# A packed attention and channel-mix kernel: the first sequence's second softmax by token, its mixing on TensorE, and another order of the first loads

## The chip, the cores and the metric

One core of a Trainium2 chip runs the whole program. Its engines work through instruction lists of their own: TensorE (PE; matmuls, with weight loads shown as PEld), VectorE (DVE), ScalarE (ACT), GpSimd (POOL) and SyncE (SP), which here issues all DMA transfers. The metric is the device time of one execution in microseconds; less is better.

## The reference

Batch 8, 8 heads, 576 tokens, head size 64, 32 packed queries p; d_model 512, d_ff 1024. All data is 32-bit float, except the weights w_k, w_v, w_r, which come in 64 bits.

```python
def sm_attn(qq, kk, vv):
    s = scale * np.matmul(qq, kk.transpose(0, 1, 3, 2))
    s = s - np.max(s, axis=-1, keepdims=True)
    a = np.exp(s)
    a = a / (np.sum(a, axis=-1, keepdims=True) + 1e-09)
    return np.matmul(a, vv)
p_packed = sm_attn(p, k, v)
x = sm_attn(q, p_packed, p_packed)          # heads side by side: 512 columns
...
xk = mu_k * x + (1.0 - mu_k) * x_prev       # x_prev: x one token earlier, 0 at the first
xr = mu_r * x + (1.0 - mu_r) * x_prev
k = np.maximum(xk @ w_k, 0.0)
v = k * k @ w_v
r = 1.0 / (1.0 + np.exp(-(xr @ w_r)))
return (r * v)
```

## The kernel before

The channel mix walks over 9 tiles of 512 tokens. For each it does gates (xr by w_r, L717 to L719), keys (xk by w_k, L678 to L680) and values (squared keys by w_v, L746 to L748): 48, 96 and 96 matmuls, since each operand is kept as a high and a low float32r half and a product takes three matmuls. Below, three matmuls of this kind are a group. Weights arrive as 64-bit blocks of 128 rows and 512 columns (`st`, 0.524 MB) and go through `convert`: ACT scales the upper words (L285), DVE puts the bits together (L287 to L291), ACT rounds to the high half (L295), DVE subtracts for the low half (L297). There are 4 blocks of w_r, 8 of w_k and 8 of w_v.

The attention of the 8 sequences is laid between these matmuls. A sequence b loads k, v, q (`raw`, `vt`, `vl`) and p (`pin`); for b = 0 and 1, k and q are transposed on PE (L387). `front` makes the first softmax and the packed keys `pm`; `back` does the second softmax with heads and packed positions on the partitions, in two halves of the tokens: scores (L541), a transpose of 32x32 blocks (L553), maximum, subtraction, exp, sum and division by packed position (L560 to L572), a transpose back (L576), and the product with `pm` (L584). `mixed_in` copies x to `xt`, and `mix` makes xr and xk: ACT scales x (L639), DVE adds the scaled x one token earlier (L643), ACT rounds (L659), DVE subtracts (L661).

The order on every engine is fixed at build time by a planner, the class `Flow`. Each piece of work is a generator that yields (engine, duration, ready time); `Flow.run` always takes the piece that could start first by its own cost figures, with a `rank` to decide ties. SP's list, and so the order of the transfers, comes out of the same planner. While the first tile is not ready, the planner fills PE with matmuls of no use (L817, `spare`). Buffers come from numbered slots, and an instruction that needs a slot waits for the last reader of the slot before.

## Time and profile before

| | us |
|---|---|
| runs | 605.92, 607.71, 608.11 |
| median | 607.71 |
| profiled execution, span from first to last instruction | 605.1 |
| PE, DVE, ACT busy in it | 593.7, 363.9, 331.0 |

The profiled execution's own device time is not given apart from its span. Times in the rows below are us from the span's start. Matmuls overlap at their ends: one of 512 columns is shown with 0.39 us, but in a stream a new one starts every 0.2275 us. A float32 matmul has two records, a transpose one.

### The profile page before, as it was taken

How to read it: one execution, taken by the hardware profiler on the slowest of the kernel's cores; microseconds unless marked ns; L12 is line 12 of the kernel's file. 1: busy time of each engine (PE TensorE's matmuls, PEld its weight loads, DVE VectorE, ACT ScalarE, POOL GpSimd, SP SyncE). 2: the span in 40 equal slices, each digit the busy share in tenths (PEclk: the TensorE clock that was granted, in tenths of full speed). 3: DMA queues.
4: the chain of work that ended last, by engine and by line, in shares of the span. 5: the costliest groups of instructions: out<-in, count | busy, mean ns of one | idle time of the engine just before them, and what ended most of it. 6: DMA issues, size and time to landing. Idle time of an engine off the chain costs nothing.

```text
span 605.1 us, 10174 instructions
## 1 busy us (share of the span) xinstructions
PE 593.7 (98%) x3984; PEld 471.1 (78%) x3984; DVE 363.9 (60%) x701; ACT 331.0 (55%) x579; POOL 2.1 (0%) x23
## 2 busy tenths in 40 slices
PE   8899999999999999999999999999999999999997
PEld 7787777777777777777877787778788888888886
DVE  1499999949688479556765577166503822451321
ACT  4478784775774648454845485457534803641420
POOL 0000000000000000000000000000000000000000
PEclk9899999999999999999999999999999999999999
DMA  8895561764634646346034702000010010001001
GB/s 189 248 266 136 216 155 34 166 126 88 113 60 137 118 70 139 99 74 143 1 103 64 144 1 72 20 1 0 26 45 1 0 70 0 2 0 71 0 2 69
DMA packets 159184, 49.43 MB, mean 82 GB/s; under 512 B 143776, under 2 KB 151968, under 8 KB 159136
## 3 DMA queue, kind: packets, MB, share of 16 engines
q1 hardware_dynamic: 159136, 48.79, 34.0%
q8 instruction: 31, 0.51, 0.3%
q14 instruction: 17, 0.14, 0.1%
HBM read 39.33 MB, written 9.44 MB: 81 GB/s over the span
## 4 chain that ended last, share of the span: by engine, by line
PE 84%; DVE 5%; ACT 4%; SPq 3%; DMA 2%; issue 1%; ACTq 0%
PE pvo L746 11%; PE ph L678 10%; PE pvo L747 10%; PE pvo L748 10%; PE ph L680 10%; PE ph L679 10%; PE pr L717 5%; PE pr L719 5%; PE pr L718 5%; SPq L207 3%; PE pa L461 2%; PE pa L584 2%; DMA st<-in_moe_w_r 1%; PE pa L541 1%; ACT x L639 1%; DVE m L289 1%
## 5 line engine op out<-in xcount | busy, mean ns | idle before, releaser
L678 PE MATMUL ph<-xk,wk_h 128*128 128x512 f32 x288 | 114.8, 399 | 0.0
L746 PE MATMUL pvo<-wv_h,sq 128*128 128x512 f32 x288 | 113.9, 395 | 0.0
L679 PE MATMUL ph<-xk,wk_h 128*128 128x512 f32 x288 | 112.4, 390 | 0.0
L680 PE MATMUL ph<-xk,wk_l 128*128 128x512 f32 x288 | 112.3, 390 | 0.0
L747 PE MATMUL pvo<-wv_l,sq 128*128 128x512 f32 x288 | 112.3, 390 | 0.0
L748 PE MATMUL pvo<-wv_h,sq 128*128 128x512 f32 x288 | 112.2, 390 | 0.0
L689 ACT ACTIVATE r<-ph 128x512 f32<-128x512 f32 x72 | 43.0, 598 | 90.7 <-PE ph L680 89.7
L696 DVE CAST sq<-r 128x512 fp32r<-128x512 f32 x72 | 30.3, 420 | 100.6 <-ACT r L692 98.4
L746 PEld LDWEIGHTS pvo<-wv_h,sq 128*128 128x128 f32 x288 | 54.1, 188 | 15.9 <-issue 4.5
L678 PEld LDWEIGHTS ph<-xk,wk_h 128*128 128x128 f32 x288 | 54.1, 188 | 15.5 <-issue 4.5
L643 DVE SCALAR_TENSOR_TENSOR x<-xt,mus,x 128x512 f32<-128x512 f32 (+7 forms) x128 | 60.4, 513 | 6.0 <-ACT x L639 5.9
L680 PEld LDWEIGHTS ph<-xk,wk_l 128*128 128x128 f32 x288 | 54.1, 188 | 11.5
L748 PEld LDWEIGHTS pvo<-wv_h,sq 128*128 128x128 f32 x288 | 54.1, 188 | 11.4
L639 ACT ACTIVATE x<-xt,mus 128x512 f32<-128x512 f32 (+7 forms) x128 | 62.0, 530 | 1.5 <-DVE xr L661 1.3
L747 PEld LDWEIGHTS pvo<-wv_l,sq 128*128 128x128 f32 x288 | 54.1, 188 | 10.7
L679 PEld LDWEIGHTS ph<-xk,wk_h 128*128 128x128 f32 x288 | 54.2, 188 | 10.3
L717 PE MATMUL pr<-wr_h,xr 128*128 128x512 f32 x144 | 58.7, 408 | 0.0
L719 PE MATMUL pr<-wr_h,xr 128*128 128x512 f32 x144 | 56.7, 394 | 1.0 <-DVE xr L661 1.0
L718 PE MATMUL pr<-wr_l,xr 128*128 128x512 f32 x144 | 56.3, 391 | 0.0
L728 ACT ACTIVATE sig<-pr 128x512 f32<-128x512 f32 x36 | 21.3, 601 | 60.1 <-PE pr L719 56.5
L698 DVE TENSOR_TENSOR sq<-r,sq 128x512 fp32r<-128x512 f32 x72 | 49.4, 686 | 1.4
L757 DVE TENSOR_TENSOR sig<-pvo,sig 128x512 f32<-128x512 f32 x36 | 23.9, 686 | 38.8 <-PE pvo L748 38.8
(80 smaller groups left out, 727.5 us busy)
## 6 DMA issues: line engine op xcount, KB each, us to landing
out<-sig SPq DMA_DIRECT2D x36, 256.0 KB, 2.1
vt<-in_v SPq DMA_DIRECT2D x16, 512.0 KB, 4.6
raw<-in_k SPq DMA_DIRECT2D x96, 72.0 KB, 2.8
raw<-in_q SPq DMA_DIRECT2D x96, 72.0 KB, 2.8
st<-in_moe_w_k SPq DMA_DIRECT2D x8, 512.0 KB, 6.0
st<-in_moe_w_v SPq DMA_DIRECT2D x8, 512.0 KB, 5.5
raw<-in_k SPq DMA_DIRECT2D x16, 144.0 KB, 2.9
raw<-in_q SPq DMA_DIRECT2D x16, 144.0 KB, 5.1
```

What stands on the lines that cost most here:

```text
L639: nc.scalar.mul(x32[:, o:o + n], xts[b, c][:, 1 + s:1 + s + n], mus[:, j, c:c + 1])
L643: nc.vector.scalar_tensor_tensor(x32[:, o:o + n], xts[b, c][:, s:s + n], mus[:, j + 1, c:c + 1], x32[:, o:o + n], op0=ALU.mult, op1=ALU.add,)
L678: nc.tensor.matmul(ph, wk_h[:, c, fs], xh, start=(c == 0), stop=False)
L679: nc.tensor.matmul(ph, wk_h[:, c, fs], xl, start=False, stop=False)
L680: nc.tensor.matmul(ph, wk_l[:, c, fs], xh, start=False, stop=(c == NC - 1))
L698: nc.vector.tensor_tensor(hl[:, 1, :], r, hl[:, 0, :].bitcast(F32), op=ALU.subtract)
L717: nc.tensor.matmul(pr, xh[:, ts_], wr_h[:, c, :], start=(c == 0), stop=False)
L718: nc.tensor.matmul(pr, xh[:, ts_], wr_l[:, c, :], start=False, stop=False)
L719: nc.tensor.matmul(pr, xl[:, ts_], wr_h[:, c, :], start=False, stop=(c == NC - 1))
L746: nc.tensor.matmul(pv[t], sh, wv_h[:, f, :], start=(f == 0), stop=False)
L747: nc.tensor.matmul(pv[t], sh, wv_l[:, f, :], start=False, stop=False)
L748: nc.tensor.matmul(pv[t], sl, wv_h[:, f, :], start=False, stop=(f == NF - 1))
```

## The change

For sequence 0 the second softmax puts tokens on the partitions: `both` holds the packed keys of each pair of heads apart, scores come out as 128 tokens by 8 heads by 32 positions (`by_token`), the softmax runs along the free dimension (`weights_by_token`, three windows of 256, 256 and 64 tokens), and PE transposes the weights to `A0`. Then xr and xk of tile 0 come straight from PE: `shared` multiplies `pm` by mu and 1 - mu, and `first_mix` adds the product with `A0` and that with `A0` one token earlier in PSUM, 256 tokens at a time; `first_out` rounds and subtracts from there. The 64 tokens that belong to tile 1 are kept aside.

The planner's constants change the order of the loads. Blocks of weights have buffers of their own (`st`, 8); the split w_v is written over its own block; w_k's conversions wait for the last window of `A0` (`held`). The shares mu are loaded as rows and transposed on PE for the later tiles, and broadcast to 32 partitions for sequence 0; those loads and sequence 0's pins are issued on POOL.

```diff
-    FIRST = 10.09, 10.29
+    FIRST = 9.985, 9.995, 9.997, 10.06
...
+        if beside:
+            yield "gpsimd", 1.0, None, None
+            nc.gpsimd.dma_start(dst, src)
+            return
...
+        if held:
+            yield from flow.wait(("A", 2))
...
+        if hi is None:
+            wv = wvs[c] = tile_([P, 2, DM], F32R, "st", slot, "wv")
+            h, l = wv[:, 0, :], wv[:, 1, :]
...
+    def by_token(sb2, both):
...
+                    nc.tensor.matmul(
+                        s2[:n, j, :, 32 * pr:32 * pr + 32], ts["qT", 0, pr][1][:, t:t + n], both[:, :, pr, :],
+                        start=True, stop=True,
+                    )
...
+    def weights_by_token(w, blocks, slot, s2):
...
+        nc.vector.tensor_reduce(m2, sc, axis=AX.X, op=ALU.max)
+        nc.vector.tensor_tensor(e, sc, m2.unsqueeze(3).broadcast_to([n, nb, 8, 32]), op=ALU.subtract)
+        nc.scalar.activation(e, e, AF.Exp, scale=scale)
+        nc.vector.tensor_reduce(z2, e, axis=AX.X, op=ALU.add)
...
+        nc.vector.tensor_tensor(e, e, z2.unsqueeze(3).broadcast_to([n, nb, 8, 32]), op=ALU.mult)
...
+        nc.scalar.copy(parts["A0"][:, :, 1 + t:1 + t + total], tp[:, :, :total])
...
+    def first_mix():
...
+                for tap in range(2):
+                    for pr in (2 * g, 2 * g + 1):
+                        own = slice(32 * pr, 32 * pr + 32)
+                        for h, half in enumerate(HALVES):
+                            o = 1 - tap + t
+                            nc.tensor.matmul(
+                                px[half, pr % 2, :n], pms[own, j, tap, h * D:(h + 1) * D], A[own, h, o:o + n],
+                                start=(tap == 0), stop=(tap == 1),
+                            )
...
+    def first_out(tag, j, w, g, slot, px, tiles, kept):
...
+            nc.scalar.copy(tiles[c][:, 0, cols], px[:, c % 2, :n])
+            nc.vector.tensor_tensor(tiles[c][:, 1, cols], px[:, c % 2, :n], tiles[c][:, 0, cols].bitcast(F32), op=ALU.subtract)
```

SP's list at the first loads, before (`st` are weight blocks, `mus` the shares, `pin` the p of the next sequence):

```order
L207 DMA vt<-in_v 128x4x256
L207 DMA vl<-in_v 64x4x64
L207 DMA raw<-in_q 96x6x64 x8
L207 DMA st<-in_moe_w_r 128x1024 x2
L207 DMA mus<-in_moe_mu_k 128x4x1
L207 DMA mus<-in_moe_mu_r 128x4x1
L207 DMA st<-in_moe_w_r 128x1024 x2
L207 DMA pin<-in_p 32x4x32 x3
L207 DMA st<-in_moe_w_k 128x1024
```

And SP's list now, from the last of sequence 0's k on:

```order
L212 DMA st<-in_moe_w_r 128x1024
L212 DMA vt<-in_v 128x4x256
L212 DMA vl<-in_v 64x4x64
L212 DMA vt<-in_v 128x4x256
L212 DMA vl<-in_v 64x4x64
L212 DMA st<-in_moe_w_r 128x1024 x2
L212 DMA raw<-in_q 96x6x64 x8
L212 DMA st<-in_moe_w_r 128x1024
L212 DMA by_row<-in_moe_mu_k 4x128
L212 DMA by_row<-in_moe_mu_r 4x128
L212 DMA st<-in_moe_w_k 128x1024 x8
L212 DMA pin<-in_p 32x4x32 x4
```

Three blocks of w_r moved ahead of q, all of w_k ahead of the next sequence's pins, and sequence 0's own pins left SP.

DVE's list at the end of the second softmax of sequence 0, now (`et` are weights by token, `m2t` their maxima and sums, `pt` the transposed pins of sequence 1):

```order
L657 TENSOR_REDUCE m2t<-s2t 64x8
L669 RECIPROCAL m2t<-m2t 128x16
L659 TENSOR_TENSOR et<-s2t,m2t 64x256
L671 TENSOR_TENSOR et<-et,m2t 128x512
L665 TENSOR_REDUCE m2t<-et 64x8
L752 TENSOR_TENSOR xr<-pa,xr 128x256
L667 TENSOR_SCALAR m2t<-m2t 64x8
L425 STREAM_TRANSPOSE pt<-pin 128x128
L752 TENSOR_TENSOR xr<-pa,xr 128x256 x2
L669 RECIPROCAL m2t<-m2t 64x8
L671 TENSOR_TENSOR et<-et,m2t 64x256
L752 TENSOR_TENSOR xr<-pa,xr 128x256 x4
```

Before, that transpose (L416) stood far behind, among the keys; now it stands between the first subtractions of xr (L752).

PE's list at the first gates, now (L731 is the mixing product, L677 the transposes of the weights):

```order
L731 MATMUL pa<-A_403,pms 64x256 x16
L677 MATMUL tpt<-ident,et 128x128 x4
L1022 MATMUL spare<-ident 128x128 x4
L731 MATMUL pa<-A_403,pms 64x256 x8
L897 MATMUL pr<-wr_h,xr 128x512
L898 MATMUL pr<-wr_l,xr 128x512
L899 MATMUL pr<-wr_h,xr 128x512
L731 MATMUL pa<-A_403,pms 64x256 x8
L677 MATMUL tpt<-ident,et 128x64 x2
L897 MATMUL pr<-wr_h,xr 128x512
```

Mixing products now stand between the groups of gates, where fillers stood; sequence 1's transposes of k, which all came before the gates, now come among the last gates and the first keys.

## Rows read from the trace of the kernel before

**Rows 1.** The page, parts 1 and 2: busy time of every engine, and TensorE's busy tenths in 40 slices of 15.1 us.

```profile
PE 593.7 (98%) x3984; PEld 471.1 (78%) x3984; DVE 363.9 (60%) x701; ACT 331.0 (55%) x579; POOL 2.1 (0%) x23
...
PE   8899999999999999999999999999999999999997
```

**Rows 2.** The table of stages (busy us of each engine and instructions in a stretch, granted TensorE clock, busy share of the DMA engines, GB/s), for the scaling stage of tile 0 and for the end of its values.

```profile
40.00:50.00 10.00, 9.02 (x73) 8.06 (x72) 9.93 (x17) 9.82 (x19) 0.00 (x0) 1.00 0.99 267
100.00:120.00 20.00, 20.00 (x140) 14.70 (x139) 20.00 (x41) 13.72 (x29) 0.10 (x1) 1.00 0.51 120
```

**Rows 3.** PE's timeline from the last transposes of sequence 0's keys to the scores of sequence 1 (start, us, instruction, idle time before it in brackets with its releaser).

```profile
7.62 0.69 PE L387 MATMUL pa<-ident,raw 96*128 96x96 f32 x6 [0.18 <-DMA raw<-in_k]
...
44.67 0.48 PE L717 MATMUL pr<-wr_h,xr 128*128 128x512 f32 x1
...
48.56 2.39 PE L817 MATMUL spare<-ident 128*128 128x128 f32 x20
...
52.33 0.48 PE L717 MATMUL pr<-wr_h,xr 128*128 128x512 f32 x1
...
61.57 0.39 PE L678 MATMUL ph<-xk,wk_h 128*128 128x512 f32 x1
...
70.56 1.21 PE L437 MATMUL pa<-kT,pt 64*32 64x288 f32 x32 [1.34 <-DVE pt L416]
```

**Rows 4.** The line that issues all loads, L207, in three stretches: durations of the issue (min/median/max in ns), first and last start, and the time from issue to landing (the last pin of sequence 0; the last two pieces of q; all pieces of q to 60 us).

```profile
L207 SPq DMA_DIRECT2D pin<-in_p x1: 429/429/429, 6.5 to 6.5; - x1
...
DMA to landing us min/median/max: 1.7/1.7/1.7
...
L207 SPq DMA_DIRECT2D raw<-in_q x2: 429/468/506, 16.4 to 16.9; - x2
...
DMA to landing us min/median/max: 2.9/3.6/4.2
...
L207 SPq DMA_DIRECT2D raw<-in_q x14: 376/518/3148, 9.5 to 46.2; - x14
```

**Rows 5.** The table of stages for the time of the loads; the last two columns are the busy share of the DMA engines and GB/s.

```profile
10.00:15.00 5.00, 4.50 (x50) 3.86 (x34) 1.94 (x6) 2.29 (x6) 0.00 (x0) 1.00 0.96 236
15.00:20.00 5.00, 3.35 (x57) 2.98 (x57) 0.00 (x0) 1.96 (x6) 0.00 (x0) 0.82 0.85 180
20.00:30.00 10.00, 10.00 (x140) 8.76 (x139) 6.70 (x13) 4.94 (x12) 0.00 (x0) 0.92 0.88 285
24.00:26.00 2.00, 2.00 (x42) 1.45 (x27) 1.97 (x3) 0.94 (x2) 0.00 (x0) 1.00 1.00 404
```

**Rows 6.** ACT's timeline while q arrives: the copy of the transposed packed keys, the first step of a weight block, and a copy of a half of q.

```profile
22.64 0.28 ACT L485 COPY ppT<-pa 128x128 f32<-128x128 f32 x1
22.80 0.69 ACT L285 ACTIVATE m<-st 128x512 f32<-128x512 f32 x1
23.37 0.41 ACT L392 COPY qT<-pq 128x288 f32<-128x288 f32 x1
```

**Rows 7.** DVE's timeline: the transpose of sequence 0's pins, two maxima of the second softmax, a subtraction and two scaled additions of the mixing, and the first and last step of one w_k block.

```profile
8.34 0.31 DVE L416 STREAM_TRANSPOSE pt<-pin 128x128 f32<-128x128 f32 x1 [8.34 <-DMA pin<-in_p]
...
26.68 1.37 DVE L560 TENSOR_REDUCE m<-e 128x18 f32<-128x576 f32 x2
...
45.61 0.69 DVE L661 TENSOR_TENSOR xr<-x,xr 128x512 fp32r<-128x512 f32 x1
...
49.34 1.41 DVE L643 SCALAR_TENSOR_TENSOR x<-xt,mus,x 128x512 f32<-128x512 f32 x2
...
55.28 0.42 DVE L287 TENSOR_SCALAR m<-m 128x512 uint32<-128x512 uint32 x1
...
57.07 0.68 DVE L297 TENSOR_TENSOR wk_l<-m,wk_h 128x512 fp32r<-128x512 f32 x1
```

**Rows 8.** PE's timeline at two places where small matmuls stand inside the stream: three transposes of q among the keys, and one output product of sequence 1 among the values (16 records are 8 matmuls).

```profile
76.36 0.39 PE L680 MATMUL ph<-xk,wk_l 128*128 128x512 f32 x1
76.59 0.41 PE L387 MATMUL pa<-ident,raw 96*128 96x96 f32 x3
...
77.10 0.40 PE L679 MATMUL ph<-xk,wk_h 128*128 128x512 f32 x1
...
101.60 0.39 PE L748 MATMUL pvo<-wv_h,sq 128*128 128x512 f32 x1
101.92 0.74 PE L584 MATMUL pa<-a,pm 32*64 32x288 f32 x16
...
102.92 0.40 PE L747 MATMUL pvo<-wv_l,sq 128*128 128x512 f32 x1
```

**Rows 9.** The table of stages around the wait for q; the third column from the end is the granted clock as a share of 2.4 GHz.

```profile
14.00:16.00 2.00, 0.49 (x5) 0.23 (x3) 0.00 (x0) 0.60 (x2) 0.00 (x0) 1.00 0.44 98
16.00:17.00 1.00, 0.35 (x3) 0.28 (x3) 0.00 (x0) 0.00 (x0) 0.00 (x0) 1.00 1.01 229
19.00:20.00 1.00, 1.00 (x8) 0.92 (x6) 0.00 (x0) 0.60 (x3) 0.00 (x0) 0.50 0.84 163
22.00:23.00 1.00, 1.00 (x13) 1.00 (x11) 0.00 (x0) 0.94 (x4) 0.00 (x0) 1.00 0.72 178
```

**Rows 10.** The timeline of all engines at the first gates of tile 1: the subtraction that makes the last xr tile, and the matmul that reads it.

```profile
120.23 0.69 DVE L661 TENSOR_TENSOR xr<-x,xr 128x512 fp32r<-128x512 f32 x1
...
121.06 0.41 PE L719 MATMUL pr<-wr_h,xr 128*128 128x512 f32 x1
```

More of the change, by code (lines that the diff above doesn't have):

```diff
@@ L213, in attn_pack_channel_mix @@
     LANDS = 2.0
+    WLOAD = 2.6e-3
     T6 = S // 6
@@ L482, in front @@
         nc.tensor.transpose(pT[:, :P], pm.rearrange("p a b -> p (a b)"), ident)
+        if b == 0:
+            s2 = yield from flow.take("a2")
+            both = tile_([P, 2, NPR, 32], F32, "a2", s2, "ppB")
+            nc.gpsimd.memset(both, 0.0)
+            yield act(2 * P)
+            for h, own in enumerate(HALVES):
+                nc.scalar.copy(both[own, h], pT[own, :P].rearrange("p (r x) -> p r x", x=32))
+            flow.give("pa", slot)
+            flow.spawn(shared(sp, pm), RANK_MIX)
+            parts["A"] = yield from flow.take("xt")
+            A = parts["A0"] = tile_([P, 2, S + 1], F32, "xt", parts["A"], "A0")
+            nc.gpsimd.memset(A[:, :, 0:1], 0.0)
+            flow.spawn(by_token(s2, both), rank(b) - 1)
+            return
         ppT = sb.tile([P, P], F32, name="ppT", tag="ppT")
@@ L593, in back @@
             flow.spawn(mixed_in(b, hf, g, slots[g], px[g]), rank(b, hf) - 1)
+    parts = {}
+    WINDOWS = (0, 256), (256, 256), (TB, S - TB)
+    def by_token(sb2, both):
+        yield from flow.wait(*(("qT", 0, pr) for pr in range(NPR)))
+        todo = []
+        for w in range(3):
+            slot = yield from flow.take("m")
+            s2 = ps.tile([P, 2, 2, P], F32, name="s2t", tag=f"m{slot}")
+            blocks = [(t, min(P, S - t)) for t in range(256 * w, min(256 * w + 256, S), P)]
+            yield pe(0.55 * len(blocks))
+            for j, (t, n) in enumerate(blocks):
+                for pr in range(NPR):
+                    nc.tensor.matmul(
+                        s2[:n, j, :, 32 * pr:32 * pr + 32], ts["qT", 0, pr][1][:, t:t + n], both[:, :, pr, :],
+                        start=True, stop=True,
+                    )
+            flow.spawn(weights_by_token(w, blocks, slot, s2), rank(0) - 1 + 0.001 * w if w < 2 else RANK_MIX + 0.02)
+        for pr in range(NPR):
+            flow.give("kq", ts.pop(("qT", 0, pr))[0])
+        flow.give("a2", sb2)
@@ new lines, in shared @@
+    def shared(sp, pm):
+        yield from flow.wait("mub")
+        ss = yield from flow.take("sig")
+        parts["pms"] = ss
+        pms = parts["pm"] = tile_([P, 2, 2, 2 * D], F32, "sig", ss, "pms")
+        flat = pm.rearrange("p a b -> p (a b)")
+        for j in (1, 0):
+            yield vec(P)
+            nc.vector.tensor_tensor(pms[:, j, 0], flat, mub[1][:, j], op=ALU.mult)
+            yield vec(P)
+            nc.vector.tensor_tensor(pms[:, j, 1], flat, pms[:, j, 0], op=ALU.subtract)
+        flow.give("pm", sp)
+        flow.give("sig", mub[0])
+        flow.set("pms")
@@ L629, in mix @@
         for c in range(NC):
-            yield from flow.wait(*(("xt", b, c, hf) for b, *_ in pieces(i) for hf in range(2)))
+            yield from flow.wait(*(
+                e for b, *_ in pieces(i)
+                for e in ([("xt", b, c, 0), ("xt", b, c, 1)] if b else [("kept", j // 2, c // 2)])
+            ))
             slot = yield from flow.take("xk" if tag == "xk" else "sq")
-            space = "sig" if i == 0 else "tmp"
+            space = "tmp"
             sx = yield from flow.take(space)
@@ L666, in attn_pack_channel_mix, with made @@
     sqs, sigs = {}, {}
+    def made(tag, i, c, t=NT - 1):
+        if i:
+            return [(tag, i, c)]
+        return [(tag, 0, c, hf) for hf in range(1 + (t >= 2))]
     def keys(i):
@@ L712, in gates @@
             for c in range(NC):
-                yield from flow.wait(("xr", i, c), *(("wr", c, o) for o in range(0, DM, WP)))
+                yield from flow.wait(*made("xr", i, c, t), *(("wr", c, o) for o in range(0, DM, WP)))
                 yield pe(0.69)
@@ L785, in all_loads @@
             yield from loads(b)
+    mub = []
     def shares():
-        for j, mu in ((0, mu_k), (2, mu_r)):
-            yield from load(mus[:, j, :], mu.rearrange("(c p) -> p c", p=P), 0.46, 0.23)
+        sm = yield from flow.take("sig")
+        mub[:] = sm, tile_([P, 2, 2 * D], F32, "sig", sm, "mub")
+        for j, mu in ((0, mu_k), (1, mu_r)):
+            for pr in range(NPR):
+                yield from load(
+                    mub[1][32 * pr:32 * pr + 32, j, :],
+                    mu[2 * D * pr:2 * D * (pr + 1)].unsqueeze(0).broadcast_to([32, 2 * D]), 0.46, 0.05, beside=True,
+                )
+        flow.now.t += 2.5
+        flow.set("mub")
+        flow.now.t = 0.0
+        flow.now.rank = RANK_SHARES
+        sr = yield from flow.take("tmp")
+        by_row = tile_([2 * NC, P], F32, "tmp", sr, "by_row")
+        for j, mu in ((0, mu_k), (1, mu_r)):
+            yield from load(by_row[NC * j:NC * (j + 1), :], mu.rearrange("(c p) -> c p", p=P), 0.46, 0.05)
             if not j:
                 back_to_issue()
+        slot = yield from flow.take("pa")
+        pT = banks(slot).rearrange("p a b -> p (a b)")
+        yield pe(0.1)
+        nc.tensor.transpose(pT[:, :2 * NC], by_row, ident[:2 * NC, :2 * NC])
+        flow.give("tmp", sr)
+        yield act(2 * NC)
+        nc.scalar.copy(mus[:, 0::2, :], pT[:, :2 * NC].rearrange("p (a b) -> p a b", a=2))
+        flow.give("pa", slot)
         yield vec(2 * NC)
```

144 lines of the change are left out of this document (113 added, 31 removed).

## The prediction

> **What bounds the kernel now.** Five views, in this order. The page says TensorE is busy 98% of the span, with full digits from slice 3 on [rows 1]. The table of stages adds that DVE is full from 40 to 50 us and still at 100 to 120 us, while PE loses little [rows 2]. So from some moment on PE is a stream that nothing interrupts, and the end lies one stream behind that moment. PE's timeline finds it [rows 3]: gates of tile 0 begin at 44.67 us, but by 52.33 only three groups of three matmuls are done, with fillers between; from there groups follow at one matmul in 0.2275 us, and keys begin at 61.57. In the keys one wait of 1.34 us stands before the scores of sequence 1. I therefore compare "start of keys, plus what PE loses after it": before, 61.57 + 1.34 = 62.9 us. Everything behind (tiles 1 to 8, the tail) is the same work, so a microsecond here is one at the end, unless DVE turns late.
>
> **Arrival of the data.** The first 25 us wait for loads. The last of k was there at 7.6 [rows 3], the pins at 6.5 + 1.7 = 8.2, the last of q at 16.9 + 4.2 = 21.1 [rows 4]; these 12.9 us carried v and q, 1.18 MB each. At the rates of the windows around (236 and 180 GB/s, [rows 5]) it would be 5.0 + 6.6 = 11.6. I take 12.2. A weight block has 0.524 MB: 1.3 us at the best window's 404 GB/s, 1.84 at the 285 of 20 to 30 us [rows 5]; I take 1.3, because that window carried mostly weights. Afterwards three w_r blocks come before the end of q: 8.2 + 3.9 + 12.2 = 24.3 us (23.7 to 26.6), the fourth at 25.6. Eight w_k blocks (10.4) and the pins of sequence 1 (0.6 before, 0.7 here) put those pins at 36.7 us (36.1 to 43.9). I leave the small loads moved to POOL in the place of the old pins.
>
> **The chain after q.** On ACT the first step of w_r's last block stands before the last copy of q: 25.6 + 0.6 + 0.4 = 26.6 us [rows 6]. Then the scores by token run; DVE needs the first eight products. The fillers, 128 columns wide, pass at 0.12 a record, two records to a product [rows 3]; with 64 columns I put a product between 0.12 and 0.24, so the eight end at 27.6 to 28.5. Meanwhile DVE converts that block, 1.8 us [rows 7], to 28.0, and takes the list shown by the order: nine passes of 512 elements at 0.65 [rows 7], 5.9; four of 256, 1.4; five small ones, 0.7; and 0.7 for two returns from exp. It meets the transpose of sequence 1's pins at 36.7 us. The two meet; whichever is later counts, and I take 37.0. This wait is new: behind this transpose stand the subtractions that free the PSUM slots, and PE's next mixing product waits for those. Then transpose 0.25, two subtractions 0.7, one mixing product and handovers 0.75: first gate at 38.7, not 44.67.
>
> **The gates.** 48 matmuls at 0.2275 are 10.9 us. Between them now stand five mixing products of 256 columns. No row has them. The nearest is the product of 8 matmuls of 288 columns with 32 rows each: with it 1.32 us lie between the starts at 101.60 and 102.92, where two matmuls alone take 0.455, so 0.86 [rows 8]. With 256 columns that is 0.8, but only four places of the array serve here, twice; at worst each tap is a full round, 1.2; at best 0.6. I take 0.85, being nearest to that row: 4.25. Three of 64 columns at 0.4, 1.2; one transpose, 0.4. Two pieces of k's transposes at 0.28: three in a row stretch the same two from 0.455 to 0.74 [rows 8]; 0.56. Sum 17.3: keys at 56.0. In the keys follow one small product, 0.4, and six pieces of transposes, 1.7, which before were done in PE's idle time. So 58.1 against 62.9: 4.8 us gained, if the stall of 1.34 goes too. Its pins land at 37. The last k of sequence 1 takes the buffer of the first, whose transposes end near 56.5; with 2.9 to landing, the least of [rows 4], it is there at 60, and PE needs it near 61.
>
> **Two charges.** ACT has in the gates 13 casts of 256 at 0.3 (an estimate by the 288 of [rows 6]), five small copies, seven first steps and four splits of weights at 0.5 to 0.6, three sigmoids, a table load and one copy of k: some 14.5 us in 17.3, in a fixed order. Before, the same engines cost PE 52.33 - 44.67 - 9 x 0.2275 = 5.6 us [rows 3]. Bounds 0 to 5.6; I take 1.0, as the scaling and adding (eight of 0.7 on DVE, [rows 7]) are gone. And the clock: after PE worked 0.8 of 3 us at 14 to 17, the granted clock fell to 0.5, the lower of 1.2 and 2.4 GHz, and was full again at 22 to 23 [rows 9]. PE waits again, for q and for the pins. Over q this hides behind DVE; in the gates some 3.5 us at half speed lose 1.7. Bounds 0 to 1.7; I take 0.6. The net is 4.8 - 1.0 - 0.6 = 3.2 us.
>
> **The other edits.** w_v in place: same eight conversions and matmuls; its loads wait for w_k's conversion, the first at about 44 us, and are needed near 88, so nothing; without that cover a block is 1.3 us each. Shares as rows: two loads of 4 lines, off the path, nothing; the old ones were strided, and their gain is in the order above. Copying the last 64 tokens: ACT in tile 1, where it has room, nothing. DVE's whole load up to gates of tile 1 falls by about 6 us: eight additions of 0.7, eight subtractions of 0.6 and eight pieces of 0.2 go [rows 7], 16 half subtractions of 0.35 come, softmax by token costs some 7 us against 8, the shares 0.8. That matters: before, the last subtraction there ended 0.14 us before PE took it (120.92 and 121.06, [rows 10]). PE comes 3.2 us sooner, DVE about 5, so no new wait; beyond 5 us DVE caps the gain.
>
> The profiled execution has a span of 605.1 us, and 601.9 is forecast. Its own time is not given apart; the median of the runs is 607.71, 2.6 above the span, so the forecast is **604.5 us**.
>
> **Rivals.**
> *A: more is won.* Mixing at 0.6 (1.5 saved), no waits, full clock: 3.2 + 1.5 + 1.6 = 6.3, with DVE's cap some 5 to 6: 602. For it: DVE waits less than before. Against: ACT's list is 84% full.
> *B: given back.* The gates wait as long as before: 4.8 - 5.6 - 0.6 is a loss of 1.4, and half as long a gain of 1.4: 606 to 609, say 607.5. For it: both engines were full through this stage [rows 2]. Against: DVE's additions are gone.
> *C: slower by the pins.* Weights at 1.84 us each put the pins at 8.2 + 12.2 + 12 x 1.84 + 0.7 = 43.2, DVE stands at its transpose, and the gates start at 44.9, later than before. It decides from 40.2 (37.0 + 3.2); at 43.2 the time is 604.5 + 6.2 = 610.7. For it: the 285 GB/s. Against: the 404; small packets of k were mixed into the 285.
> *D: slower by POOL.* Twelve loads are issued there, one of them before the identity that all transposes need; the fourth pin is the seventh. The trace has no load issued on POOL. Nearest are SP's: 0.43 us for a pin [rows 4], at most 3.15 [rows 4]. I take 1.0, nearer to the pins' row: pins at 1.1 + 7 + 2 = 10.1, and 11.5 us later, at 21.6, the packed keys are copied: before, 14.3 us lay between the two steps, 8.34 to 22.64 [rows 6, 7], and I take 2.8 off for the waiting for v in it. This is hidden until 26.6. From 1.7 an issue it shows, from about 2.2 the gain is gone; at 3.15 the keys are 10 us late: 614.
> In the trace DVE is idle until 8.34 us [rows 7], and with the change its first instruction is the transpose that waits for these very pins; only the loads of the shares could meet a busy DVE.
> The Trainium skill (SBUF — State Buffer, sections "SBUF: two separate sides" and "A bandwidth-pool intuition that's wrong") says that a load issued on GpSimd has its descriptors written there, that a DVE instruction which uses both read ports keeps GpSimd from writing them, and that such a load took 3100 ns in place of 620. By that rule D would come wherever the two overlap, and near 614 us; no run here shows it.
>
> **Numbers.** A measurement of this kernel can tell about 0.5%, 3.0 us, from no change. Forecast 0.48 (602.5 to 606.5); A 0.20; B 0.16; C 0.09; D 0.07. Faster (under 604.7): 0.30 of the forecast's share and A, 0.50. Same: its other 0.18 and 0.14 of B, 0.32. Slower: C, D and 0.02 of B, 0.18. The range leaves out the far ends of A and of C and D: 599.5 to 610.
>
> **What would show it.** Right: the last of q near 24.3; DVE waiting for pins near 36 to 37; the first gate near 38.7; keys at 56 to 58; transposes of k inside them; no wait before sequence 1's scores; full PE behind. Wrong: pins of sequence 0 after 13 us (D) or of sequence 1 after 40 (C); fillers or gaps of over 3 us among the gates (B); mixing products over 1.2 us; idle PE at gates of tile 1, where DVE would have become the bound.

## The result, and the profile after

The changed kernel takes 610.90 us, the median of 20 runs (607.64 to 618.68); the kernel before took 606.57 beside it (20 runs, 605.11 to 610.00). The ratio is 1.0073, 95% interval 1.0047 to 1.0099: slower by 0.7%, clear of the noise, where 604.5 was forecast. Ten of the twenty runs lie at 607.6 to 610.2 us with a mean granted clock of 0.998 or more, the other ten at 611.6 to 618.7 with 0.985 to 0.992, so that the median falls into the gap between the two groups; the profiled execution (617.72) is one of the latter.

The page, parts 1 and 2, to be read against [rows 1]; the third line is the granted TensorE clock in tenths:

```profile
PE 603.6 (98%) x4065; PEld 472.5 (77%) x4065; DVE 360.0 (58%) x699; ACT 326.4 (53%) x585; POOL 8.7 (1%) x35
...
PE   8889999999999999999999999999999999999997
...
PEclk9986999999999999999999999999999999999999
```

PE is as busy as before and ten microseconds longer. The 8 and the 6 in the clock line mark the third and the fourth slice, 31 to 62 us. The table of stages, as in [rows 2, 5, 9] (stretch, its length, the busy us of PE, PEld, DVE, ACT and POOL, granted clock, share of the DMA engines, GB/s), shows it:

```profile
30.00:40.00 10.00, 9.02 (x103) 8.11 (x102) 7.39 (x18) 4.02 (x9) 0.00 (x0) 1.00 1.00 329
40.00:50.00 10.00, 8.66 (x43) 4.61 (x43) 4.43 (x12) 3.17 (x8) 0.00 (x0) 0.57 0.22 50
42.00:50.00 8.00, 8.00 (x42) 4.07 (x35) 2.70 (x7) 2.80 (x7) 0.00 (x0) 0.50 0.16 38
50.00:58.00 8.00, 8.00 (x42) 4.53 (x42) 3.83 (x9) 3.02 (x7) 0.00 (x0) 0.50 0.21 68
50.00:60.00 10.00, 10.00 (x61) 5.60 (x60) 4.34 (x9) 3.02 (x7) 0.00 (x0) 0.58 0.21 63
```

From 40 to 60 us DVE and ACT are not half busy, where both were full from 40 to 50 before; the last column but two, the granted clock, is 0.50 from 42 to 58 us, so PE runs at 1.2 GHz there. The weights of 30 to 40 us come at 329 GB/s. PE's timeline, as in [rows 3, 8]:

```profile
37.96 1.06 PE L1022 MATMUL spare<-ident 128*128 128x128 f32 x8
41.34 1.98 PE L731 MATMUL pa<-A,pms 32*64 32x256 f32 x16 [2.32 <-DVE m2t L669]
43.25 0.80 PE L897 MATMUL pr<-wr_h,xr 128*128 128x512 f32 x1
...
58.73 0.40 PE L899 MATMUL pr<-wr_h,xr 128*128 128x512 f32 x1
59.06 1.09 PE L731 MATMUL pa<-A,pms 32*64 32x256 f32 x16
...
69.78 0.48 PE L858 MATMUL ph<-xk,wk_h 128*128 128x512 f32 x1
...
77.73 1.20 PE L449 MATMUL pa<-kT,pt 64*32 64x288 f32 x32
```

PE stands empty for 2.32 us, works at half speed from there to 58, and keys begin at 69.78 in place of 61.57. The stall of 1.34 us before the scores of sequence 1 is gone, as forecast. Ahead of the empty stretch, ACT's and DVE's timelines, as in [rows 6, 7]; the first line is the first step of w_r's last block, forecast for 25.6:

```profile
27.08 0.66 ACT L288 ACTIVATE m<-st 128x512 f32<-128x512 f32 x1 [1.90 <-DMA st<-in_moe_w_r]
```

```profile
8.02 0.31 DVE L425 STREAM_TRANSPOSE pt<-pin 128x128 f32<-128x128 f32 x1 [8.02 <-DMA pin<-in_p]
...
40.24 0.31 DVE L425 STREAM_TRANSPOSE pt<-pin 128x128 f32<-128x128 f32 x1 [1.79 <-DMA pin<-in_p]
40.48 0.72 DVE L752 TENSOR_TENSOR xr<-pa,xr 128x256 fp32r<-128x256 f32 x2
```

DVE waits 1.79 us for sequence 1's pins, and behind that transpose stand the subtractions that free the PSUM slot for PE's next product. (The releaser named in PE's line, L669, is the small instruction right behind those two.) The pins are issued at 30.2 to 33.2 and land 6.9 to 9.4 us later, behind eight blocks of w_k (the line that reads them, as in [rows 4]):

```profile
L212 SPq DMA_DIRECT2D pin<-in_p x4: 312/329/495, 30.2 to 33.2; - x4
...
DMA to landing us min/median/max: 6.9/8.7/9.4
```

The chain of waits that ended last goes the same way, from the last pin's landing over DVE to PE:

```profile
33.18 6.94 DMA pin<-in_p
...
40.24 0.31 DVE pt L425
40.55 0.64 DVE xr L752 x2
...
41.34 1.98 PE pa L731 x16
```

At the gates of tile 1, DVE and PE run as closely as in [rows 10], at a later time:

```profile
130.32 0.69 DVE L835 TENSOR_TENSOR xr<-x,xr 128x512 fp32r<-128x512 f32 x1
131.06 0.50 PE L899 MATMUL pr<-wr_h,xr 128*128 128x512 f32 x1 [0.24 <-DVE xr L835]
```

### The profile page after: what moved, and what is told of

Read it like the earlier page. It is cut to its first block, busy times and chain, and to the rows that moved or that the text cites. A ratio compares the mean times of both kernels' runs of the same rounds, so it can differ in the third digit from the quotient of the medians.

```text
span 615.8 us, 10367 instructions
## 1 busy us (share of the span) xinstructions
PE 603.6 (98%) x4065; PEld 472.5 (77%) x4065; DVE 360.0 (58%) x699; ACT 326.4 (53%) x585; POOL 8.7 (1%) x35
## 3 DMA queue, kind: packets, MB, share of 16 engines
q1 hardware_dynamic: 157520, 48.72, 33.2%
## 4 chain that ended last, share of the span: by engine, by line
PE 89%; DMA 3%; SPq 3%; ACT 2%; DVE 1%; issue 0%; DVEq 0%
PE ph L858 11%; PE ph L859 11%; PE ph L860 11%; PE pvo L926 10%; PE pvo L927 10%; PE pvo L928 10%; PE pr L897 6%; PE pr L899 5%; PE pr L898 5%; SPq L212 3%; PE pa L473 2%; PE pa L731 2%; PE pa L612 2%; PE pa L569 1%; DMA st<-in_moe_w_k 1%; ACT x L807 1%
## 5 line engine op out<-in xcount | busy, mean ns | idle before, releaser
L926 PE MATMUL pvo<-wv,sq 128*128 128x512 f32 x288 | 114.1, 396 | 0.0
L927 PE MATMUL pvo<-wv,sq 128*128 128x512 f32 x288 | 112.4, 390 | 0.0
L928 PE MATMUL pvo<-wv,sq 128*128 128x512 f32 x288 | 112.3, 390 | 0.0
L876 DVE CAST sq<-r 128x512 fp32r<-128x512 f32 x72 | 30.2, 420 | 102.0 <-ACT r L872 99.7
L926 PEld LDWEIGHTS pvo<-wv,sq 128*128 128x128 f32 x288 | 54.1, 188 | 16.5 <-issue 5.0
L928 PEld LDWEIGHTS pvo<-wv,sq 128*128 128x128 f32 x288 | 54.1, 188 | 11.4
L860 PEld LDWEIGHTS ph<-xk,wk_l 128*128 128x128 f32 x288 | 54.1, 188 | 11.4
L927 PEld LDWEIGHTS pvo<-wv,sq 128*128 128x128 f32 x288 | 54.1, 188 | 10.5
L897 PE MATMUL pr<-wr_h,xr 128*128 128x512 f32 x144 | 61.1, 424 | 0.0
L813 DVE SCALAR_TENSOR_TENSOR x<-xt,mus,x 128x448 f32<-128x448 f32 (+6 forms) x112 | 53.3, 514 | 9.3 <-ACT x L807 9.0
L899 PE MATMUL pr<-wr_h,xr 128*128 128x512 f32 x144 | 57.9, 402 | 0.4 <-DVE xr L835 0.4
L898 PE MATMUL pr<-wr_l,xr 128*128 128x512 f32 x144 | 57.8, 401 | 0.0
L807 ACT ACTIVATE x<-xt,mus 128x448 f32<-128x448 f32 (+6 forms) x112 | 54.5, 528 | 1.5 <-DVE xr L835 1.5
```

Of the source, the lines that this page charges most:

```text
L807: nc.scalar.mul(x32[:, o:o + n], xts[b, c][:, 1 + s:1 + s + n], mus[:, j, c:c + 1])
L813: nc.vector.scalar_tensor_tensor(x32[:, o:o + n], xts[b, c][:, s:s + n], mus[:, j + 1, c:c + 1], x32[:, o:o + n], op0=ALU.mult, op1=ALU.add,)
L860: nc.tensor.matmul(ph, wk_l[:, c, fs], xh, start=False, stop=(c == NC - 1))
L897: nc.tensor.matmul(pr, xh[:, ts_], wr_h[:, c, :], start=(c == 0), stop=False)
L898: nc.tensor.matmul(pr, xh[:, ts_], wr_l[:, c, :], start=False, stop=False)
L899: nc.tensor.matmul(pr, xl[:, ts_], wr_h[:, c, :], start=False, stop=(c == NC - 1))
```

## The experiments

Sixteen runs. Two theories stood at the beginning: W, the wait for the pins and the empty PE behind it cost the time, and let the clock fall; M, the clock falls because the mixing products lie between the gates. All ratios below are to the kernel before, on the same chip. The table gives, from each profile, the start of the first gates, of the first keys, of the gates of tiles 1 and 2, and the span, in us; then the median of the runs and the ratio with its interval. The medians of the kernel before beside these runs were 606.2 to 606.6.

| | gates | keys | gates 1 | gates 2 | span | median | ratio |
|---|---|---|---|---|---|---|---|
| before | 44.67 | 61.57 | 118.56 | 186.19 | 605.1 | | |
| after | 43.25 | 69.78 | 127.72 | 196.21 | 615.8 | 610.90 | 1.0073 (1.0047–1.0099) |
| e0_after | 40.38 | 63.13 | 121.05 | 189.51 | 609.2 | 611.62 | 1.0078 (1.0045–1.0111) |
| e1_pins | 38.96 | 58.70 | 116.63 | 185.09 | 604.6 | 607.39 | 1.0031 (1.0009–1.0053) |
| e2_fill | 41.70 | 61.41 | 119.33 | 187.82 | 607.4 | 609.33 | 1.0050 (1.0037–1.0063) |
| e3_loads | 46.49 | 64.59 | 119.20 | 190.18 | 609.9 | 611.07 | 1.0080 (1.0065–1.0096) |
| e4_wr3 | 39.28 | 58.55 | 117.45 | 189.24 | 608.7 | 612.35 | 1.0098 (1.0082–1.0114) |
| e5_kfirst | 41.33 | 57.88 | 116.61 | 190.57 | 610.2 | 612.08 | 1.0104 (1.0088–1.0120) |
| e6_loads_pins | 48.47 | 66.25 | 119.22 | 190.19 | 609.7 | 610.95 | 1.0075 (1.0061–1.0089) |
| e7_all | 40.39 | 59.67 | 116.63 | 191.29 | 610.7 | 614.34 | 1.0141 (1.0124–1.0157) |
| e8_pins_fill | 40.03 | 59.73 | 117.67 | 186.13 | 605.6 | 607.43 | 1.0025 (1.0004–1.0045) |
| e9_before_pt | 44.07 | 60.94 | 117.96 | 185.60 | 604.5 | 606.32 | 1.0002 (0.9992–1.0011) |
| e10_wr_late | 40.24 | 60.65 | 118.05 | 185.60 | 605.2 | 609.44 | 1.0058 (1.0037–1.0078) |
| e11_among | 44.00 | 67.25 | 125.16 | 193.62 | 613.1 | 613.20 | 1.0126 (1.0090–1.0163) |
| e12_sp | 42.64 | 62.35 | 120.29 | 188.78 | 607.8 | 609.60 | 1.0070 (1.0056–1.0084) |
| e13_twice | 40.44 | 64.43 | 122.34 | 190.81 | 610.3 | 612.19 | 1.0092 (1.0078–1.0106) |
| e14_pairs | 38.38 | 53.55 | 114.83 | 185.88 | 604.9 | 609.15 | 1.0036 (1.0022–1.0051) |
| e15_merge | 43.43 | 67.15 | 126.11 | 194.49 | 612.8 | 614.76 | 1.0128 (1.0102–1.0154) |

Each row is one execution, and its start depends on when the loads came: with one and the same order of loads q's last piece landed at 23.8 us in the profile of the change, at 21.7 in e0_after and at 24.1 in e2_fill. So starts compare to about 2 us, stretches much better: from the first keys to gates 2 it is 126.4 us in eight of the profiles.

### The wait, the clock

*e0_after*: the changed kernel again, no edit.

> The changed kernel once more, unaltered. Its executions so far lie in two groups, 607.6 to 610.2 us at a mean granted clock of 0.998 or more, and 611.6 to 618.7 at 0.985 to 0.992. Both theories expect both groups again. Theory W (DVE stands at the transpose of sequence 1's pins, L425, PE runs empty for 2.3 us behind it, and that empty stretch is what lets the clock fall) expects in a profile at full clock: the wait of about 1.8 us on DVE still there, first gate at 42.3 us, keys at 62.8, span 605.7 to 607.6. Rival M (the clock falls because the mixing products, 32 rows and 64 columns each, are laid between the gates) expects the half clock wherever these products stand, and so no profile of this kernel with the products and full clock from 41 to 58 us.

Both groups came again: three of eight runs at 607.1 to 608.5 us (clock 1.0), five at 611.2 to 617.2. The profile has the wait (1.64 us on DVE, 2.17 on PE), and half clock for some 7 us. It is not the profile at full clock for which the two theories had named numbers. Its table of stages:

```profile
40.00:42.00 2.00, 2.00 (x18) 0.92 (x11) 0.74 (x3) 0.75 (x2) 0.00 (x0) 0.67 0.00 0
42.00:46.00 4.00, 4.00 (x23) 2.38 (x18) 1.62 (x5) 2.06 (x5) 0.00 (x0) 0.50 0.20 46
46.00:48.00 2.00, 2.00 (x19) 0.90 (x17) 0.36 (x1) 0.00 (x0) 0.00 (x0) 0.62 0.27 59
48.00:50.00 2.00, 2.00 (x27) 0.99 (x19) 1.26 (x3) 1.66 (x4) 0.00 (x0) 1.00 0.03 8
```

*e1_pins*: only SP's list changes.

```diff
 DMA by_row<-in_moe_mu_r
+DMA pin<-in_p x4
 DMA st<-in_moe_w_k x8
-DMA pin<-in_p x4
```

> Only the four loads of sequence 1's pins move: on SP they stand ahead of the eight w_k blocks and not behind them. All other lists are unaltered, and the weights come about 0.6 us later. W: the pins land near 29 us, DVE's wait of 1.79 us at L425 goes, PE's gap of 2.32 us shrinks below 1, first gate at 40.4 us (43.25 less 1.94 of wait and 0.9 of half clock), keys at 60.9, granted clock 1.00 from 40 to 60 us, every run at 605.0 to 607.0 and none over 610. M: the start comes 2 us sooner, but in part of the executions the clock still falls to half among the gates: runs up to 614.

*e2_fill*: ahead of the mixing product that waits,

```diff
+                for _ in range(10 if (tag, w, g) == ("xr", 1, 0) else 0): fill()
```

> Ten matmuls of no use (128 columns, 0.24 us each) are put on PE ahead of the mixing product that waits (xr, second window), so that PE works through the 2.3 us of its wait; the order of all else is unaltered and the pins come as late as before. W: the start is unchanged, first gate 42.3 us, keys 62.8, granted clock 1.00 from 40 to 60 us, all runs in 607.5 to 610.5: the slower of the two groups is gone. M: the fillers do not touch the mixing products, so part of the runs still has the half clock and 611 to 617 us.

*e8_pins_fill*: e1_pins with `range(3 ...)` of the same line.

> e1_pins with three matmuls of no use (0.24 us each) ahead of the mixing product before which PE was still idle for 0.43 us. In e1_pins 2 of 12 runs showed the lower clock (0.984 and 0.989; 614.6 and 616.2 us). W: with the last gap filled no run lies below 0.996, the others stay where they were: 606.4 to 608.5 us. M (the products among the gates lower the clock): 1 or 2 runs of 12 again above 612.

In e1_pins DVE meets its transpose without a wait, at 36.86 us, and PE's gap is 0.43 (DVE's and PE's timelines):

```profile
36.86 0.30 DVE L436 STREAM_TRANSPOSE pt<-pin 128x128 f32<-128x128 f32 x1
```

```profile
37.94 1.09 PE L742 MATMUL pa<-A,pms 32*64 32x256 f32 x16 [0.43 <-DVE m2t L680]
38.96 0.50 PE L908 MATMUL pr<-wr_h,xr 128*128 128x512 f32 x1
...
58.70 0.48 PE L869 MATMUL ph<-xk,wk_h 128*128 128x512 f32 x1
```

The eight of its twelve runs with a clock of 0.999 or more lie at 606.5 to 608.0 us, 607.0 in the middle, against 608.8 for the ten such runs of the changed kernel, and 608.5 for the three of e0_after, which ran beside e1_pins: the late pins cost 1.4 to 1.8 us, and they are not all of the loss. In e2_fill all six runs show 0.998 or more, with the products where they were; if ten in twenty fell as before, six without a fall would be one chance in 64. So filling the gap takes the group at the lower clock away, and the products alone don't make it. (e2_fill's fillers end at 40.67, half a microsecond after the subtractions that free PE's slot, so that much of its start is theirs.) The clock is not settled altogether. e1_pins has two runs at 0.984 and 0.989 (616.15 and 614.57 us), where W expected none over 610, and e8_pins_fill has one of twelve at 0.989 (614.26), which is what M expected there and not W. Hardly any gap is left in these two kernels, no profile caught such a run, and what made the clock fall in them stays open.

*e11_among*: the gap stays, six matmuls of no use behind three of the mixing products.

```diff
+                for _ in range(6 if (tag, w, g) in (("xr", 1, 0), ("xr", 1, 1), ("xk", 0, 0)) else 0): fill()
```

> The changed kernel with its late pins and its gap, and six matmuls of no use (1.4 us) behind each of three mixing products among the first gates. It asks why the clock stays at half for 7 to 17 us in e0_after's and the changed kernel's profiles, and for 3 us in e3_loads, whose gap is as long but whose gates stand between such matmuls. If the mixing products (32 rows by 64 columns) keep it low: runs with a drop show mean clocks of 0.994 to 0.997, and all runs lie in one band, 609.5 to 613.5 us. If not: two groups again, 611.5 to 614 at full clock and 615 to 622 at 0.985 to 0.992.

Five of six runs show 0.996 to 1.0 (611.9 to 615.0), one 0.988 (619.5). In its profile the gap is 2.85 us and the clock is low for about 3.5 us; in e3_loads, with 1.99 us and fillers behind, for about 3.5 too. Among the products it was 7 and 17. So the products seem to hold it low once it has fallen. Six runs with one exception don't prove it, and by the times the case without this effect fits as well: four runs at 611.9 to 613.5, one at 619.5 with 0.988.

### What the order of loads costs

*e3_loads* and *e6_loads_pins*: the new loads (SP's list, POOL, buffers, w_v in place, w_k held until the mixing of the second half) under the old softmax and the old mixing, of which the core is below; e6 with SP's edit of e1_pins.

```diff
-    FIRST = 10.09, 10.29
+    FIRST = 9.985, 9.995, 9.997, 10.06
+        if held:
+            yield from flow.wait(("px", 0, 1))
...
-                0.63, 0.1,
+                0.63, 0.1, beside=(b == 0),
```

> The changed order of loads alone: pins of sequence 0 on POOL, shares as rows, w_r ahead of q, weight blocks in buffers of their own, w_v in place, w_k's conversion held back; the second softmax and the mixing of tile 0 are those of the kernel before, and the shares for 32 partitions are not loaded, since nothing needs them. If the loss lies in the order of loads (q's last piece at 24.9 us in place of 21.1, pins at 40.2): first gate at 46 us or later, keys at 62 to 65, 607 to 611 us. If the loss lies in what the change lays between the gates (five mixing products of about 1.2 us, and transposes of k moved into the keys): first gate at 43 to 45, keys at 59 to 61.5 and no transposes of k in the keys, 604 to 606.5 us.

> As e3_loads (the new order of loads alone, 611.07 us), but with sequence 1's pins ahead of w_k on SP. If the pins are the whole of what the new order of loads costs: PE's wait of 1.99 us at the second mixing product goes, the first gate comes from 46.49 to about 44.5 us, keys from 64.6 to 61.5 to 62.5, and the time is 606 to 608. If the w_r blocks ahead of q cost it as well (q's scores begin at 25.5 us and not at 22): 608.5 to 610.5.

The new order of loads alone makes the kernel 0.8% slower, as much as the whole change, and moving the pins doesn't mend it: e6_loads_pins lies above both of its ranges, since PE waits 2.17 us for the k of sequence 1 instead, which now comes behind w_k. On these loads the softmax by token and the mixing on PE therefore gain, 611.1 (all runs) to 608.8 (those at full clock); but w_k's conversions are held by another event in e3_loads, so the difference isn't theirs alone.

*e10_wr_late*: e1_pins with two blocks of w_r behind q.

```diff
-    FIRST = 9.985, 9.995, 9.997, 10.06
+    FIRST = 9.985, 10.06, 10.06, 10.06
```

> e1_pins with two of the three w_r blocks that the change put ahead of q loaded behind it again, so q comes 2.7 to 3.7 us sooner (last transposes near 21.5 us). If q's arrival sets the start: first gate near 36.5 us, keys at 56.5, 605 us. If DVE's work sets it (two conversions of 2.4 us now fall behind q): first gate at 38.5 to 41, keys at 58.5 to 61, 607 to 609 us. A wait of PE at the gates of tile 1 of over 1 us, as in e4_wr3, would add to either.

q's last transposes come at 23.59 us in place of 24.19, not at 21.5. Gates at 40.24 and keys at 60.65 are the second case, DVE's work: nothing is won at the start. *e12_sp*: e1_pins with the twelve loads of POOL on SP.

```diff
-            nc.gpsimd.dma_start(dst, src)
+            nc.sync.dma_start(dst, src)
```

> e1_pins, but the twelve loads that the change issues on POOL (pins of sequence 0, shares for 32 partitions) are issued on SP, between the first loads of k, v and q; every other list is unaltered. In all profiles of kernels that issue on POOL, 4.2 to 4.5 us pass from PE's end to the end of the span, in the kernel before and e9_before_pt 3.7, and the fillers begin at 2.5 us in place of 1.5. If the loads on POOL cause this, the end part is 3.7 us here, the identity is there at 1.5, and the time falls by 0.5 us from e1_pins' 607.1, to 606.6. If SP's list is what the loads of k, v and q wait for, twelve issues of about 0.45 us delay q by up to 5 us and the time rises to 609 to 612.

The second case: the pins of sequence 0 come late (PE waits 3.77 us for them), q's last transposes begin at 27.87, and the time is 609.6. So the issues on POOL save some 2.5 us. The first case stays open: behind PE's end 3.8 us pass here, 3.7 before and in e9_before_pt, and 4.2 to 4.5 in all but one of the kernels that issue on POOL; but that one, e14_pairs, has the same twelve loads on POOL and 3.8.

### What a product costs, and what a start is worth

*e13_twice*: e1_pins with five products done twice.

```diff
-                for tap in range(2):
+                twice = w < 2 and (tag, w) != ("xr", 0) and (tag, w, g) != ("xr", 1, 0)
+                for tap in (0, 1, 0, 1) if twice else (0, 1):
```

> e1_pins with the five mixing products of 256 tokens that lie among the gates of tile 0 done twice each (the second time over the first, with the same result). It measures the price of the term that was put at 0.85 us a product. If a product costs PE what the profile shows (1.2 us of extra distance between the gates around it): 607.1 + 6 = 613.1 us, first keys near 64.7. If 0.85: 611.4. If part of it is hidden, because the gates wait for ACT and DVE anyway: under 610.

*e14_pairs*: e1_pins, both head groups of a window behind each other.

```diff
-            for g in range(2):
-                slot = yield from flow.take("pa")
+            slots = yield from two_slots()
+            for g in range(2):
```

> e1_pins with the mixing products issued in pairs (both head groups of one window behind each other). In e13_twice a product directly behind another cost 0.87 us, while one alone among gates costs 1.22 in e1_pins, so each way into the small tiles and back costs about 0.35 us. Five pairs in the place of ten single products among gates and keys save five such ways: 607.1 - 1.75 = 605.3 us. Rival: a pair needs both PSUM slots free, so the pair before must have gone through ACT and DVE, and PE waits for that in the gates; or DVE is late at the gates of tile 1, as in e4_wr3 (2.4 us): 607 to 611 us.

PE's timeline around one product in e1_pins, around one done twice in e13_twice, and around a pair in e14_pairs:

```profile
42.41 0.40 PE L910 MATMUL pr<-wr_h,xr 128*128 128x512 f32 x1
42.73 1.09 PE L742 MATMUL pa<-A,pms 32*64 32x256 f32 x16
43.75 0.50 PE L908 MATMUL pr<-wr_h,xr 128*128 128x512 f32 x1
44.09 0.40 PE L909 MATMUL pr<-wr_l,xr 128*128 128x512 f32 x1
```

```profile
44.74 0.40 PE L911 MATMUL pr<-wr_h,xr 128*128 128x512 f32 x1
45.07 1.96 PE L743 MATMUL pa<-A,pms 32*64 32x256 f32 x32
46.96 0.50 PE L909 MATMUL pr<-wr_h,xr 128*128 128x512 f32 x1
47.29 0.39 PE L910 MATMUL pr<-wr_l,xr 128*128 128x512 f32 x1
```

```profile
43.78 0.39 PE L911 MATMUL pr<-wr_h,xr 128*128 128x512 f32 x1
44.10 1.22 PE L742 MATMUL pa<-A,pms 32*64 32x256 f32 x32
45.25 0.50 PE L909 MATMUL pr<-wr_h,xr 128*128 128x512 f32 x1
45.59 0.40 PE L910 MATMUL pr<-wr_l,xr 128*128 128x512 f32 x1
```

From the first row to the last, less two matmuls of 0.2275: 1.22 us for a product, 2.10 for one done twice, 1.36 for a pair. The second product on the same rows adds 0.87; the one of the other head group adds 0.14, which fits that it lies in other rows of the array and runs beside the first. (The repeated product also writes the same PSUM tile again; no run parts the two.) What is left of 1.22, some 0.35, I read as the way into the small tiles and back. The Trainium skill (TensorEngine Tiling (Array Packing), section "Key Properties") says both: tiles work independently of each other, and a change of the tiling mode drains TensorE; the rows agree.

A product has eight matmuls on four places of the array, one round for each tap, so 0.87 is two rounds of 0.435. The product of [rows 8] has eight matmuls on eight places, one round of 288 columns: 0.35 + 0.435 x 288/256 = 0.84, measured 0.86. And with 64 columns two rounds give 0.35 + 0.22 = 0.57, measured 0.58. One sum fits all three.

From first gates to first keys e13_twice takes 24.0 us and e1_pins 19.7, which is 4.25 more, about five times 0.87; from the keys to gates 2 both take 126.4. Its median is 4.8 us above e1_pins', between the cases of 0.85 and of 1.2. So the products lie on the path with their full price.

In e14_pairs the keys begin at 53.55 us, 5.15 sooner than in e1_pins and 8 sooner than before the change. Some 2.3 us of the 5.15 are work that only moved: three products of 64 tokens and two transposes of k (3 x 0.58 + 2 x 0.28), ahead of the first keys in e1_pins, stand behind them here. Gates 1 are 1.8 us sooner than in e1_pins. Nothing of it arrives: gates 2 are 0.8 later, and the time is not better. PE's waits from 64 to 300 us (us in total, how often, the longest), against 0.6 in e1_pins:

```profile
PE pr L911 <- DVE xr L847: 1.5, 3, 0.8
PE pr L909 <- ACT xr L845: 0.7, 1, 0.7
PE pa L558 <- ACT qT L414: 0.6, 1, 0.6
PE pa L405 <- ACT a L548: 0.3, 1, 0.3
```

The chain of waits lies on PE from 37.9 to 82 us in e1_pins, and on DVE from 40 to 73 in e14_pairs. So DVE and ACT take the end over when PE comes sooner, while a later start arrives in full: those 126.4 us from keys to gates 2 are the same for keys at 58.70 and at 69.78.

*e9_before_pt*: the kernel before, one instruction earlier on DVE.

```diff
+L586 STREAM_TRANSPOSE pt<-pin 128x128
 L587 STREAM_TRANSPOSE a_543<-e 128x576
...
-L416 STREAM_TRANSPOSE pt<-pin 128x128
```

> The kernel before, with one instruction moved on DVE: the transpose of sequence 1's pins stands ahead of the last transpose of sequence 0's softmax weights, and not behind w_k's conversions. It tests a term of the prediction, that PE's wait of 1.34 us before sequence 1's scores is worth 1.34 us at the end. If so, 606.2 - 1.3 + 0.3 (the transpose now lies in DVE's full stretch before the gates) = 605.2 us, and no wait before the scores. Rival: DVE, whose last xr of tile 1 was ready 0.14 us before PE took it, turns late at the gates of tile 1, and the time stays at 606.2.

The rival came: the stall of 1.34 us is gone, and the time is the same to 0.1%. PE's timeline shows a wait that takes its place:

```profile
68.52 1.20 PE L444 MATMUL pa<-kT,pt 64*32 64x288 f32 x32
...
75.29 0.47 PE L387 MATMUL pa<-ident,raw 96*128 96x96 f32 x3 [0.59 <-ACT a L517]
```

The scores come 2.04 us sooner than before, the transposes of q behind them 1.30, and from 79 us on all is 0.6 sooner, which was there at the keys already. The rival had looked for DVE at the gates of tile 1; the wait stands earlier, on ACT.

*e4_wr3* (e1_pins, the last w_r block converted once A0's second window stands), *e5_kfirst* (e1_pins, `et` in the `e` buffers, three pieces of sequence 1's k loaded ahead of w_k) and *e7_all* (both, with four fillers):

```diff
+                flow.spawn(convert(w_r, wr_h, wr_l, c, o, WP, ("wr", c, o), first.pop(0) if first else None, held=("A", 1) if c == 3 else None), RANK_W)
...
+                if b == 1: flow.now.rank = 13.55 if tag == "kT" and pr < 3 else LOADS_1
+        e = tile_([P, 2, 8, 32], F32, "e", se, "et")[:n, :nb]
```

> As e1_pins (pins of sequence 1 ahead of w_k), and the conversion of the last w_r block is held back until the second window of the softmax weights stands in A0; its load keeps its place. Theory: DVE's list between q and the first gates sets the start (in e1_pins PE's last wait is still on DVE, 0.43 us), so taking 2.4 us of conversion out of it brings the first gate from 38.96 to about 36.8 us, keys from 58.7 to 56.5, and the time from about 607.1 (the middle of e1_pins' runs at full clock) to 605. Rival: the conversion is late for the fourth group of gates; PE waits or falls in step with DVE there, keys stay at 58 to 59 us and the time at 607.

> As e1_pins, and the softmax weights by token use the e buffers, so that three of the four k pieces of sequence 1 can be loaded ahead of w_k and are transposed while PE still runs fillers. Theory: the later loss is PE's own work that before lay in its idle time: six pieces of transposes leave the gates and keys, 1.7 us, and the time falls from 607.1 to about 605.4. Rival: the 3 us by which w_k comes later are needed, keys wait for w_k or DVE, and the time stays at 607 or rises.

> e4_wr3 and e5_kfirst together, with four more matmuls of no use ahead of the third mixing product. If the effects add: 607.1 - 2.2 - 1.7 = 603.2 us, and with the gap filled every run at a mean clock of 0.998 or more. If only one of the two holds: 605 to 605.5. Rival: without w_r's last block and k's transposes in the way, DVE's conversions of w_k become the limit, keys stand behind w_k, and the time stays at 606 to 607 as before the change.

None of the three theories held: gates come no sooner than in e1_pins, and 3 to 6 us are lost behind gates 1 (487.97 us from there to the end in e1_pins, 491.3 to 494.1 here), where PE waits for DVE's and ACT's xr (2.4 us in e4_wr3, 3.5 in e5_kfirst, 3.9 in e7_all). The rival of e5_kfirst had foreseen a time of 607 or more, by waits in the keys. All three also let the planner order much else anew, so they show that the stage is sensitive, not the price of their one edit. *e15_merge* (e1_pins, mixed in windows of 256 and 320 tokens, in pairs) is no better:

```diff
-    WINDOWS = (0, 256), (256, 256), (TB, S - TB)
+    WINDOWS = (0, 256), (256, S - 256)
```

> e14_pairs with the last 64 tokens taken into the second window: products of 320 columns in place of 256 and 64. Four products of 64 columns (0.55 us each among gates and keys) go, four become 64 columns wider (0.2 us each, a quarter of the 0.87 of 256): 605.3 - 1.4 = 603.9 us. Rivals as for e14_pairs, and the second window of xr now waits for the last softmax weights: a wait of PE at the third tile of gates, or later keys, would give this back, 605 to 610 us.

PE waits 3.71 us for k of sequence 1 at 43 us and 3.66 for ACT at 66. No kernel here beats the one before.

## Why the prediction was wrong, point by point

Four steps failed: the price of a weight block, and with it the pins' arrival; the price of a mixing product; the credit for the stall, where PE's stream was taken for the path; and the price of the clock.

**The arrival.** q was right: its last piece, forecast for 24.3 us, landed at 23.8 (issued at 19.9, 3.9 to landing), in e0_after and e1_pins at 21.7 and 21.8. The weights were not: a block was put at 1.3 us, by the best window [rows 5]; at the 329 GB/s of 30 to 40 us it takes 1.59. Eight blocks are 2.3 us more, w_r's last block was 1.5 late as well, and the pins, put at 36.7, came at 40.2 (38.3 in e0_after). This is rival C in part: it named the wait, its place and its condition; by its own sum the gain is used up at 40.2, and it had a chance of 0.09. That its 610.7 is nearly the measured median is luck: it goes with pins at 43.2 and counts 0.6 for the clock.

**The chain after q** was right to about 1 us: from the first step of w_r's last block to DVE's arrival at the transpose 11.1 us were forecast (25.6 to 36.7) and 11.4, 11.9 and 12.5 came (the change, e0_after, e1_pins). Without late pins (e1_pins) DVE stands at its transpose at 36.86 us, forecast 37.0, and the first gate at 38.96, forecast 38.7. So close a hit is luck in part, since q landed 2.5 us sooner there than forecast.

**The gates** were put at 17.3 us and take 19.7 at full clock (e1_pins 38.96 to 58.70, e2_fill 41.70 to 61.41). The term that was mis-sized is the mixing product: put at 0.85, it costs 1.22, five times; the small ones cost 0.58, not 0.4 (in the profile of the change, 65.34 to 66.38 us less two matmuls). The 0.85 came from the product of [rows 8], whose 0.86 holds the way in and out already, but one round only. The prediction had seen that here "only four places of the array serve", twice, had named 1.2 for two full rounds as the worst case, and chose the nearer row over it; the worst case came. That 0.87 is the price of the two rounds without the way in and out is a coincidence. The charge for DVE and ACT, 1.0, was not needed.

**The credit for the stall**, 1.34 us, was wrong as a step: "start of keys, plus what PE loses after it" took PE's stream for the path. e9_before_pt shows that this stall is worth nothing, e14_pairs that PE's lead over e1_pins of 1.8 us at gates 1 is not either. The cap that I put at "some 5 to 6" us of gain lies lower: no kernel here has gates 2 more than 1.1 us sooner than the one before. The chain of waits of the kernel before could have told it. From 29 to 82 us no work of PE stands on it: it runs through DVE's and ACT's softmax, mixing and conversion of weights, a load of w_v, and DVE again:

```profile
30.53 1.41 DVE z L566 x2
...
48.89 0.61 ACT x L639
...
61.85 0.63 ACT wk_h L295
...
62.93 6.66 DMA st<-in_moe_w_v
69.60 0.68 DVE sq L698
...
79.13 0.61 DVE wv_l L297
```

**The clock**, 0.6 us, is the other mis-sized term: nothing in half of the runs and several microseconds in the rest. From first gates to first keys the profile of the change takes 26.5 us, e2_fill 19.7: 6.8 us, where 1.7 was the bound. I bounded it by the 3.5 us of [rows 9], where fillers stood behind the gap; here it stayed low for 17 us, among products. That they hold it low is probable and not shown.

**The sum.** 601.9 was forecast for the span. At full clock (e2_fill, pins still late): gates 3.0 later than forecast, 2.4 longer, no charges (-1.6), from keys to gates 2 126.4 us in place of 124.6 - 1.3 + 2.1 = 125.4 (+1.0, not traced to its parts), behind PE's end 0.6 more: 607.3; the profile has 607.4. The base was high too: before's profiled span was 605.1, and its later runs have their middle at 606.2 to 606.6 us, not 607.71.

**The rest.** Rival D did not come: the loads took 0.50 to 0.67 us of POOL each, the last pin was issued by 5.5 us, and DVE's first instruction stood at 8.02. DVE's next instructions came after POOL's last issue, so the rule of the Trainium skill (SBUF — State Buffer, section "A bandwidth-pool intuition that's wrong") was not put to the test. Rival B's place was right and its cause wrong: ACT and DVE idled there. w_v in place cost no wait: no product of the values waits in the profile of the change.
